# Loading one tile of x ahead of the last chunk of wk, and reordering the first key and query products to match

## The chip, the cores and the metric

The kernel runs on one core of a Trainium2 chip. The metric is the device time of one execution in microseconds (us), less being better. PE is the tensor engine, DVE the vector engine, ACT the scalar engine, and SP the engine that issues most of the DMA loads.

## The reference

A gated mix of two blocks over the same sequence of 2048 rows of width 640. The change touches only the first few microseconds of the attention block: the keys and queries of the first four tiles of 128 rows.

```
qkv = x @ wqkv                       # x 2048x640, wqkv 640x1920, bf16
phi = lambda t: where(t > 0, t + 1, exp(t)) + 1e-6
pq, pk = phi(q), phi(k)              # linear attention with 32 heads of 20
...
return g * a + (1 - g) * b           # g = sigmoid(x . gate_w), b = GeGLU feed-forward
```

The weights wk and wq are 640x640 slices of wqkv. They arrive in five chunks of 128 rows ("chunk 0" to "chunk 4"), because a product over 640 is five accumulated matmuls over 128.

## The kernel before

Loads. `load_xT` is a DMA that transposes a tile of x on its way; `load_wk` and `load_wq` are plain loads of one 160 KB chunk. SP issues in program order, unless `"act"` is given.

```
load_x(0); load_wk(0); load_xT(1); load_wk(3); load_wk(4)
load_wk(1, "act"); load_wk(2, "act")
...                                   # cut: gate weights, by ACT
for i in range(2, NQ):                # NQ = 4: tiles 2 and 3 of x
    load_xT(i)
for k in range(KC):                   # KC = 5
    load_wq(k)
for i in range(NQ, NT):
    load_xT(i)
```

Products. `KM(n, ks)` multiplies tile n by the chunks `ks` of wk, as a 512-wide and a 128-wide matmul per chunk; `QM` does the same with wq (its narrow half is 129 wide, by a gate column that `gate_col()` makes). Products accumulate in PSUM (`ps` in the timelines, where every matmul writes to it). It is used as four slots of two banks; keys of tiles 0 to 3 take slots 0 to 3, and then the queries of tiles 0 to 3 take the same slots again. ACT and DVE turn a finished slot into phi (`phi1`, `phi2`), after which its banks are free.

```
warm(5, 512); warm(1, 128)            # dummy products
...                                   # cut: tile 0 is transposed by PE
warm(2, 128)
for k in range(3): KM(0, [k])
for k in range(3): KM(1, [k])
KM(0, [3]); KM(1, [3])
gate_col()
KM(0, [4]); KM(1, [4])
for n in range(2 * NQ):
    if n in (2, 3):
        KM(n, ALLK)
    if n == NQ:
        for k in ALLK:
            QM(NQ, [k]); QM(NQ + 1, [k])      # two query tiles, chunk by chunk
    if n > NQ + 1:
        QM(n, ALLK)
    phi1(n); phi2(n)
for i in range(NQ, NT):
    KQ(i)                             # the combined key/query stage, tiles 4 to 15
```

One program operation waits for everything it reads at its start: `QM(n, ALLK)` waits for all five chunks of wq, `QM(n, [k])` for chunk k alone.

## Time and profile before

| | before |
|---|---|
| time, median of 6 runs | 274.07 us (273.92 to 274.27) |
| span of the profiled run | 272.6 us |
| first real product | 4.45 us |
| hole before tile 2's keys | 7.55 to 8.12 us |
| queries start | 10.85 us |
| combined stage starts | 16.30 us |

Four lines of the page: the span, PE's busy time, the busy tenths of the DMA engines in 40 slices of 6.8 us, and the chain of work that ended last, by engine.

```profile
span 272.6 us, 3416 instructions
...
PE 267.6 (98%) x1341; PEld 127.9 (47%) x1367; DVE 140.8 (52%) x247; ACT 75.9 (28%) x132; POOL 30.0 (11%) x28
...
DMA  7976999600200011514121221273031110110211
...
PE 96%; DMA 1%; SPq 1%; issue 1%; DVE 0%
```

PE is the bottleneck: 98% busy, and 96% of the chain. The loads of this change fall in the first two slices, where the DMA engines are busy to 70% and over 90%. Summed over shorter stretches, their busy share is 1.09 from 4 to 8 us and 0.91 from 8 to 12 us (a packet is counted where it starts, so a share can exceed 1). A share of about 1 is what "full" means below.

The timeline of PE in the kernel before (start, duration, engine, source line, operation, output from input, count, and in brackets the idle time with what released it). Lines 453 and 454 are the two widths of a key product, 468 and 469 those of a query product, 539 is the combined stage.

```profile
7.00 0.38 PE L453 MATMUL ps<-pool 128*128 128x512 bf16 x1
...
7.27 0.38 PE L453 MATMUL ps<-pool 128*128 128x512 bf16 x1
7.49 0.22 PE L454 MATMUL ps<-pool 128*128 128x128 bf16 x1
8.12 0.39 PE L453 MATMUL ps<-pool 128*128 128x512 bf16 x1 [0.42 <-DMA pool<-in_A_x_dram]
...
10.85 0.38 PE L468 MATMUL ps<-pool 128*128 128x512 bf16 x1
...
16.24 0.22 PE L469 MATMUL ps<-pool 128*128 128x129 bf16 x1
16.30 0.81 PE L539 MATMUL ps<-pool 128*128 128x512 bf16 x3
```

Key products of one chunk start 0.27 us apart. The last one of tile 1 starts its narrow half at 7.49, so tile 2's first would follow at 7.55, but it starts at 8.12: a hole of 0.57 us, ended by a DMA of x. (The bracket says 0.42 because the end that the profile gives a matmul is later than the start of the next: 7.27 + 0.38 = 7.65, against 7.49. I count starts.) From 10.85 the ten chunks of two interleaved query tiles and ten more follow without a hole, 20 x 0.272 = 5.45 us, until 16.30.

SP's queue in the kernel before: the time it takes to issue each load.

```profile
1.71 1.30 SPq L353 DMA_TRANSPOSE pool<-in_A_x_dram  x1
3.06 1.04 SPq L341 DMA_DIRECT2D pool<-in_A_wqkv_dram  x2
4.14 2.53 SPq L353 DMA_TRANSPOSE pool<-in_A_x_dram  x2
6.72 2.48 SPq L341 DMA_DIRECT2D pool<-in_A_wqkv_dram  x5
```

A transposing load takes SP about 1.26 us to issue (two in 2.53), a plain chunk about 0.5 (two in 1.04, five in 2.48).

The landing of a load is the moment at which the last of its 16 semaphore increments is recorded. In the kernel before, in us: wk3 6.37, wk4 6.83, x tile 2 8.07, x tile 3 8.77, wq chunks 0 to 4 at 9.40, 10.13, 10.55, 11.54 and 12.05.

### The profile page before, as it was taken

The page shows a single profiled execution, that of the slowest core. Times are in us where ns is not written, and L with a number is a line of the kernel's source. Part 1 is how long each engine was busy: PE and PEld are TensorE (multiplying, and loading weights), DVE is VectorE, ACT ScalarE, POOL GpSimd, SP SyncE. Part 2 cuts the span into 40 slices and gives each one's busy share as a digit, 9 for nine tenths or more (in the row PEclk, how much of TensorE's full clock was granted, in tenths as well). Part 3 has the DMA queues.
Part 4 walks back from the last instruction along what each step waited for, and adds up shares of the span by engine and source line. Part 5 has one row for each costly group of instructions (what it writes and reads, how often), then busy time and mean ns, then how long its engine had stood idle before and what let it go on. Part 6 is the DMA issues. An engine that isn't in the chain of part 4 may idle for free.

```text
span 272.6 us, 3416 instructions
## 1 busy us (share of the span) xinstructions
PE 267.6 (98%) x1341; PEld 127.9 (47%) x1367; DVE 140.8 (52%) x247; ACT 75.9 (28%) x132; POOL 30.0 (11%) x28
## 2 busy tenths in 40 slices
PE   8999999999999999999999999999999999999997
PEld 3555555544445454444444444444444444444444
DVE  1678989997233335999999999634210000000200
ACT  2455555210422453232222233224011122121021
POOL 5000000003240002242332422000000000000000
DMA  7976999600200011514121221273031110110211
GB/s 192 202 115 127 346 399 388 140 2 19 58 19 2 23 50 51 192 34 49 26 48 25 49 48 27 60 219 105 5 77 38 41 38 19 38 41 19 58 58 41
DMA packets 42864, 23.78 MB, mean 87 GB/s; under 512 B 32223, under 2 KB 41439, under 8 KB 42719
## 3 DMA queue, kind: packets, MB, share of 16 engines
q1 hardware_dynamic: 42517, 23.22, 31.9%
q10 hardware_dynamic: 330, 0.33, 0.3%
q8 instruction: 11, 0.18, 0.3%
q14 instruction: 6, 0.05, 0.1%
HBM read 13.83 MB, written 2.63 MB: 60 GB/s over the span
## 4 chain that ended last, share of the span: by engine, by line
PE 96%; DMA 1%; SPq 1%; issue 1%; DVE 0%
PE ps L700 41%; PE ps L864 23%; PE ps L539 12%; PE ps L596 6%; PE ps L843 4%; PE ps L468 2%; PE ps L811 2%; PE ps L678 2%; PE ps L599 1%; DMA pool<-in_A_x_dram 1%; PE ps L453 1%; PE ps L824 1%; SPq L341 1%; PE ps L721 1%; SPq L353 0%
## 5 line engine op out<-in xcount | busy, mean ns | idle before, releaser
L700 PE MATMUL ps<-pool 128*128 128x512 bf16 x510 | 113.0, 379 | 0.5
L700 PEld LDWEIGHTS ps<-pool 128*128 128x128 bf16 x520 | 50.5, 98 | 60.0
L864 PE MATMUL ps<-pool 128*128 128x512 bf16 (+2 forms) x300 | 62.4, 366 | 0.3
L706 ACT ACTIVATE pool<-ps 128x512 f32<-128x512 f32 x52 | 31.0, 597 | 73.1 <-PE ps L700 73.1
L708 DVE TENSOR_TENSOR pool<-ps,pool 128x512 bf16<-128x512 f32 x52 | 34.7, 689 | 31.7 <-PE ps L700 30.4
L864 PEld LDWEIGHTS ps<-pool 128*128 128x128 bf16 x306 | 29.2, 98 | 33.4 <-issue 0.4
L847 DVE TENSOR_TENSOR pool<-ps,pool 128x512 bf16<-128x512 f32 x4 | 2.8, 690 | 61.5 <-PE ps L843 61.5
L539 PE MATMUL ps<-pool 128*128 128x512 bf16 (+1 forms) x176 | 32.5, 343 | 0.2
L754 POOL TENSOR_TENSOR pool<-pool 128x640 f32<-128x640 bf16 x16 | 22.4, 1404 | 73.0 <-DVE pool L756 65.6
L871 ACT ACTIVATE pool<-ps,pool 128x512 bf16<-128x512 f32 (+1 forms) x16 | 10.9, 680 | 68.6 <-PE ps L864 68.6
L539 PEld LDWEIGHTS ps<-pool 128*128 128x128 bf16 x180 | 17.6, 98 | 15.0
L558 DVE SCALAR_TENSOR_TENSOR pool<-ps,pool 128x128 bf16<-128x128 f32 (+2 forms) x36 | 21.7, 602 | 2.1
L549 ACT ACTIVATE pool<-ps 128x640 bf16<-128x640 f32 x24 | 16.9, 703 | 15.8 <-DVE pool L558 9.3
L596 PE MATMUL ps<-pool 128*128 128x512 bf16 x76 | 19.2, 379 | 0.1
L764 DVE TENSOR_TENSOR pool<-pool 128x640 bf16<-128x640 bf16 x16 | 13.2, 826 | 0.6
L762 DVE TENSOR_SCALAR pool<-pool 128x32 f32<-128x32 f32 x16 | 12.8, 802 | 0.6
L756 DVE TENSOR_REDUCE pool<-pool 128x32 f32<-128x640 f32 x16 | 12.9, 808 | 0.0
L644 DVE TENSOR_TENSOR pool<-pool 128x640 f32<-128x640 f32 x14 | 11.6, 826 | 0.5
L843 PE MATMUL ps<-pool 128*128 128x512 bf16 x51 | 11.5, 379 | 0.1
L646 POOL PARTITION_ALL_REDUCE pool<-pool x1 | 4.0, 3971 | 61.0 <-DVE pool L644 61.0
L596 PEld LDWEIGHTS ps<-pool 128*128 128x128 bf16 x78 | 7.0, 98 | 7.3
L555 DVE TENSOR_SCALAR pool<-pool 128x640 bf16<-128x640 bf16 x24 | 7.9, 327 | 1.7 <-ACT pool L549 0.4
(70 smaller groups left out, 124.1 us busy)
## 6 DMA issues: line engine op xcount, KB each, us to landing
out_dram<-pool SPq DMA_DIRECT2D x19, 128.0 KB, 1.7
pool<-in_B_w_gate_dram SPq DMA_DIRECT2D x1, 2080.0 KB, 14.8
pool<-in_B_w_up_dram SPq DMA_DIRECT2D x1, 2080.0 KB, 18.0
pool<-in_A_wqkv_dram SPq DMA_DIRECT2D x8, 160.0 KB, 3.1
pool<-in_A_x_dram SPq DMA_DIRECT2D x1, 1280.0 KB, 9.2
pool<-in_A_x_dram SPq DMA_DIRECT2D x1, 1120.0 KB, 6.3
pool<-in_B_w_down_dram SPq DMA_DIRECT2D x1, 1120.0 KB, 6.4
pool<-omg_row SPq DMA_DIRECT2D x1, 1024.0 KB, 4.8
```

Source lines behind the costliest of these rows:

```text
L539: last = e.matmul(ps[:, b + p, 0:c1 - c0], xT[:, k, i * 128:(i + 1) * 128], wkq[:, k, c0:c1], start=(k == 0), stop=(k == KC - 1))
L549: P.op("act", lambda e: e.activation(e_buf[m], ps_flat[:, o:o + 640], ACT.Exp), reads=banks, writes=[r_e[m]])
L558: P.op("dve", lambda e, c0=c0, c1=c1: e.scalar_tensor_tensor(dst[:, c0:c1], ps_flat[:, o + c0:o + c1], 1.0 + EPS, e_buf[m][:, c0:c1], ALU. ...
L596: last = e.matmul(ps[:, b, :], pk[i][:, c * 128:(c + 1) * 128], x_aug[:, i, 0:512], start=(i == 0), stop=(i == NT - 1))
L700: last = e.matmul(ps[:, b, :], w[:, k, fc * 128:(fc + 1) * 128], xT[:, k, j * 512:(j + 1) * 512], start=(k == 0), stop=(k == KC - 1))
L706: P.op("act", lambda e: e.activation(ge[n], ps[:, gb, :], ACT.Gelu_apprx_tanh), reads=[bank[gb]], writes=[r_ge[n]])
L708: P.op("dve", lambda e: e.tensor_tensor(hT[fc][:, j * 512:(j + 1) * 512], ps[:, ub, :], ge[n], ALU.mult), reads=[bank[ub], r_ge[n]], write ...
L754: P.op("pool", lambda e: e.tensor_tensor(tmp[n], pq[i], z_b, ALU.mult), reads=[r_pq[i], r_zb], writes=[r_tmp[n]])
L756: P.op("dve", lambda e: e.tensor_reduce(den[n], tmp[n].rearrange("p (h d) -> p h d", h=32), AX.X, ALU.add), reads=[r_tmp[n]], writes=[r_de ...
L764: P.op("dve", lambda e: e.tensor_tensor(pq[i].rearrange("p (h d) -> p h d", h=32), pq[i].rearrange("p (h d) -> p h d", h=32), den[n].unsqu ...
L843: last = e.matmul(ps[:, b, :], wd[:, fc, 512:640], hT[fc][:, j * 512:(j + 1) * 512], start=False, stop=(fc == NFC - 2), skip_group_check=True)
L864: last = e.matmul(ps[:, pb, 0:c1 - c0], lhs, rhs, start=False, stop=(q == len(rows) - 1), skip_group_check=True)
```

## The change

The intent is to have tile 2 of x at hand when PE runs out of work, by loading it ahead of wk's chunk 4, and to do two chunks of tile 2 while chunk 4 is still on its way. The queries of the first two tiles are no longer interleaved.

```diff
             load_wk(3)
+            load_xT(2)
             load_wk(4)
+            load_xT(3)
             load_wk(1, "act")
             load_wk(2, "act")
...
-            for i in range(2, NQ):
-                load_xT(i)
             for k in range(KC):
                 load_wq(k)
...
             gate_col()
+            KM(2, [0, 1])
             KM(0, [4])
             KM(1, [4])
+            KM(2, [2, 3, 4])
             for n in range(2 * NQ):
-                if n in (2, 3):
+                if n == NQ - 1:
                     KM(n, ALLK)
                 if n == NQ:
                     for k in ALLK:
-                        QM(NQ, [k])
-                        QM(NQ + 1, [k])
-                if n > NQ + 1:
+                        QM(n, [k])
+                if n > NQ:
                     QM(n, ALLK)
```

More of the change, by code (lines that the diff above doesn't have):

```diff
@@ L347, in load_x, with load_wk, load_xT @@
                 dma_in(x_aug[:, i, 0:640], A_x[0, i * 128:(i + 1) * 128, :], [r_xn[i]], eng=eng)
-            def load_wk(k, eng="sp", after=()):
-                dma_in(wk[:, k, :], A_wqkv[k * 128:(k + 1) * 128, 640:1280], [r_wk[k]], reads=after, eng=eng)
-            def load_xT(i, after=()):
+            def load_wk(k, eng="sp"):
+                dma_in(wk[:, k, :], A_wqkv[k * 128:(k + 1) * 128, 640:1280], [r_wk[k]], eng=eng)
+            def load_xT(i):
                 P.op("sp", lambda e: e.dma_start_transpose(xT[:, :, i * 128:(i + 1) * 128],
                                                            A_x[0, i * 128:(i + 1) * 128, :]),
-                     reads=list(after), writes=[r_xT[i]], dma=new_dma_key())
+                     writes=[r_xT[i]], dma=new_dma_key())
             def load_wq(k, eng="sp"):
```

## The prediction

> **What bounds the kernel.** TensorE. The page gives PE 98% busy, the chain of waits is 96% PE[...]. From the first real matmul (4.45 us) to the last output PE has one hole worth naming: in the timeline the last key product of tile 1 starts at 7.49 us and should be out in about 0.05, and the first of tile 2 starts at 8.12, released by a DMA of x. That hole is about 0.58 us, 0.2% of the span. After it the key and query matmuls follow at 0.27 us per chunk (a 512-wide and a 128-wide product) until 16.30 us, and nothing later waits for longer than about 0.05. So what moves the start of the combined key/query stage (16.30 us) moves the end by as much.
>
> **What the change does.** No arithmetic is added or removed. SP issues x tile 2's transposing load before wk chunk 4 instead of behind it, tile 3 after chunk 4. SP issue durations in the timeline: a wk chunk 0.43-0.57 us, a transposing load about 1.26. So tile 2 is issued at 3.67 instead of 4.14, chunk 4 at about 4.95 instead of 3.67; tile 3 and wq chunks 0-4 are issued when they were. PE does two chunks of tile 2 (0.54 us) before chunk 4 of tiles 0 and 1 and the other three after; queries of tile 4's slot run alone instead of interleaved with the next one, so wq is consumed at 0.27 us per chunk instead of 0.54.
>
> **Landings now (semaphore landings of the trace), us.** wk3 6.37, wk4 6.83, xT2 8.07, xT3 8.77, wq0-4 9.40, 10.13, 10.55, 11.54, 12.05. DMA engines are near saturated over these microseconds (DMA row 7-9 tenths)[...] (SP's loads land in issue order). So swapping the two should swap about 0.46 us (wk4's step after wk3): estimate xT2 at 7.4-7.7, wk4 at about 8.1 (issue 4.95 plus the 3.16 it took).
>
> **Critical path after.**
> - Gate column ends at 7.0; PE waits for xT2 until about 7.6: a new 0.6 us hole, earlier.
> - Two chunks of tile 2, until 8.15; wk4 is there or nearly.
> - 2 chunks (tiles 0, 1), 3 of tile 2, 5 of tile 3 = 2.7 us: queries start at about 10.8 (10.85 now). Gain 0 to 0.25.
> - Query chunk 4 of the first tile is wanted at about 11.9, before wq4 lands (12.05): a new wait of 0.1-0.3 us. Queries then end at 12.05+0.27+3x1.36 = 16.4 instead of 16.30.
> The hole moves rather than closes. Net about 0, -0.3 to +0.3. ScalarE and VectorE exponentials (0.70 and 1.15 us per tile, against 1.36 of PE) start some 0.9 us later but free banks in time.
>
> **Prediction:** 274.1 us, 80% range 273.7 to 274.5; faster by over 2% 0.01, within 2% 0.98, slower 0.01.
>
> **What would show it.** The hole before tile 2's keys starts near 7.0 and ends at xT2's landing (7.4-7.7); little or no hole before chunk 4 of tile 0; a small wait on a wqkv DMA in the first query tile near 11.8; combined stage starts at 16.2-16.5; unchanged after.
>
> **What would make it wrong.** If xT2 lands by 7.2 and wk4 by 7.8, and wq4 comes earlier than 11.7, up to 0.5 us is gained. If the transposing load delays chunk 4 beyond 8.5, or wq lags more, it loses that much.

The trace of before holds no clock record. The sum came to a net of about 0, -0.3 to +0.3 us, on the 274.07 measured before. That tile 2 and chunk 4 would swap their landings was my estimate, from loads that land in the order of issue in that trace (wk3 6.37, wk4 6.83, x tile 2 8.07).

## The result, and the profile after

| | before | after |
|---|---|---|
| median of 6 runs | 274.07 us | 274.33 us |
| range of fast runs | 273.92 to 274.27 | 274.24 to 274.37 |
| ratio of fast runs, 95% interval | | 1.0008 (0.9995 to 1.0022) |

A ratio is the mean time of one kernel's fast runs over that of the other's fast runs of the same rounds, so it is not quite the ratio of the medians quoted. The change is the same within 2%, and even zero lies inside the interval.

One of the changed kernel's six executions, the profiled one, was slow (284.62 us). Its matmuls of 128x512 in the longest group take 391 ns in place of 379 ns, and the groups of the other stages are slower too. (A clock of 1.0 is given for it, but its trace holds no clock record at all, and time without a record is counted as 1.0.) I explain no time by that run. The profile after is therefore that of the same kernel run again, which is the first experiment, e1_after_again. The two traces agree in the order of the landings and in the places of the waits, but not in their size: in the slow one, queries start at 10.90, wq's chunk 4 lands at 12.15 and PE waits 0.14 us for it, where e1, read below, has 0.70 us of waits for wq. So e1 is one execution, and not the typical one.

The page of the changed kernel: the lines that answer to those of before.

```profile
span 273.2 us, 3416 instructions
...
PE 267.9 (98%) x1341; PEld 127.7 (47%) x1367; DVE 141.0 (52%) x247; ACT 75.9 (28%) x132; POOL 30.0 (11%) x28
...
DMA  7997999500300011523121221263031110110211
...
PE 94%; SPq 3%; DMA 1%; issue 1%; DVE 0%
```

The span is 0.6 us longer in this execution. PE's share of busy time did not move in a visible way, nor did the DMA row; the shares cannot show an effect of this size. The chain gives SP's queue 3% where it was 1%: before, the chain ran back to the load of x tile 2, which SP issued at 4.14 us; now it runs back to the load of wq's chunk 4, issued at 8.83, with more of SP's queue ahead of it.

The timeline of PE in the changed kernel (line 540 is the combined stage now).

```profile
7.03 0.38 PE L453 MATMUL ps<-pool 128*128 128x512 bf16 x1
...
7.30 0.38 PE L453 MATMUL ps<-pool 128*128 128x512 bf16 x1
7.52 0.22 PE L454 MATMUL ps<-pool 128*128 128x128 bf16 x1
8.00 0.39 PE L453 MATMUL ps<-pool 128*128 128x512 bf16 x1 [0.27 <-DMA pool<-in_A_wqkv_dram]
...
10.73 0.38 PE L468 MATMUL ps<-pool 128*128 128x512 bf16 x1
...
11.49 0.22 PE L469 MATMUL ps<-pool 128*128 128x129 bf16 x1
11.74 0.39 PE L468 MATMUL ps<-pool 128*128 128x512 bf16 x1
11.97 0.22 PE L469 MATMUL ps<-pool 128*128 128x129 bf16 x1
12.53 0.39 PE L468 MATMUL ps<-pool 128*128 128x512 bf16 x1 [0.34 <-DMA pool<-in_A_wqkv_dram]
...
16.84 0.22 PE L469 MATMUL ps<-pool 128*128 128x129 bf16 x1
16.90 0.59 PE L540 MATMUL ps<-pool 128*128 128x512 bf16 x2
```

The two chunks of tile 2 start at 7.03 and 7.30, right behind the gate column: tile 2 had landed at 6.87, and there is no wait for it. The hole is now at 7.57 to 8.00 us, before chunk 4 of tile 0, and is ended by a DMA of wqkv. Queries start at 10.73, which is 0.12 us earlier than before. Then they stop twice in the first tile: chunk 3 would follow at 11.55 and starts at 11.74, chunk 4 would follow at 12.02 and starts at 12.53, released by a DMA of wqkv. That is 0.19 + 0.51 = 0.70 us. The combined stage starts at 16.90: 10.73 + 5.45 + 0.70 = 16.88 accounts for it.

SP's queue in the changed kernel.

```profile
1.71 1.31 SPq L353 DMA_TRANSPOSE pool<-in_A_x_dram  x1
3.06 0.57 SPq L341 DMA_DIRECT2D pool<-in_A_wqkv_dram  x1
3.67 1.21 SPq L353 DMA_TRANSPOSE pool<-in_A_x_dram  x1
4.92 0.57 SPq L341 DMA_DIRECT2D pool<-in_A_wqkv_dram  x1
5.54 1.21 SPq L353 DMA_TRANSPOSE pool<-in_A_x_dram  x1
6.79 2.47 SPq L341 DMA_DIRECT2D pool<-in_A_wqkv_dram  x5
```

Tile 2 is issued at 3.67 in place of 4.14, and chunk 4 at 4.92 in place of 3.67. Landings in this trace: wk3 6.20, x tile 2 6.87, wk4 7.96, x tile 3 8.68, wq chunks 0 to 4 at 10.06, 10.54, 10.97, 11.70 and 12.48.

**The end follows the start of the combined stage.** Of every profiled run in the fast state, the device time minus the start of the combined stage is the same: 273.97 - 16.30 = 257.67 before, 274.49 - 16.90 = 257.59 after, and 257.58 to 257.68 in ten of the eleven others (257.82 in e7). So nothing behind the stage reacts to the change, and the start of the stage can be read as the time of the run. That gives a finer measure than the timed rounds, though of one execution each, and the stages below are compared across chips, which the times are not.

### The profile page after: what moved, and what is told of

The parts are those of the page before. It is cut to its first block, busy times and chain, and to the rows that moved or that the text cites. A ratio compares the mean times of both kernels' runs of the same rounds, so it can differ in the third digit from the quotient of the medians.

```text
span 283.4 us, 3416 instructions
## 1 busy us (share of the span) xinstructions
PE 278.7 (98%) x1341; PEld 130.6 (46%) x1367; DVE 142.2 (50%) x247; ACT 76.0 (27%) x132; POOL 30.0 (11%) x28
## 4 chain that ended last, share of the span: by engine, by line
PE 96%; SPq 1%; DMA 1%; issue 1%; DVE 0%
PE ps L701 41%; PE ps L865 23%; PE ps L540 12%; PE ps L597 6%; PE ps L844 4%; PE ps L468 2%; PE ps L812 2%; PE ps L679 2%; PE ps L600 1%; DMA pool<-in_A_wqkv_dram 1%; SPq L353 1%; PE ps L453 1%; PE ps L825 1%; PE ps L722 1%; SPq L341 0%
## 5 line engine op out<-in xcount | busy, mean ns | idle before, releaser
L701 PE MATMUL ps<-pool 128*128 128x512 bf16 x510 | 117.6, 391 | 0.6
L701 PEld LDWEIGHTS ps<-pool 128*128 128x128 bf16 x520 | 51.6, 100 | 63.5
L865 PE MATMUL ps<-pool 128*128 128x512 bf16 (+2 forms) x300 | 64.9, 377 | 0.4
L709 DVE TENSOR_TENSOR pool<-ps,pool 128x512 bf16<-128x512 f32 x52 | 35.8, 689 | 35.3 <-PE ps L701 32.6
L865 PEld LDWEIGHTS ps<-pool 128*128 128x128 bf16 x306 | 29.8, 100 | 35.4 <-issue 0.4
L848 DVE TENSOR_TENSOR pool<-ps,pool 128x512 bf16<-128x512 f32 x4 | 2.8, 692 | 64.2 <-PE ps L844 64.2
L540 PE MATMUL ps<-pool 128*128 128x512 bf16 (+1 forms) x176 | 33.7, 352 | 0.2
L540 PEld LDWEIGHTS ps<-pool 128*128 128x128 bf16 x180 | 17.9, 100 | 15.9
L597 PE MATMUL ps<-pool 128*128 128x512 bf16 x76 | 19.9, 391 | 0.1
L844 PE MATMUL ps<-pool 128*128 128x512 bf16 x51 | 12.0, 391 | 0.1
L597 PEld LDWEIGHTS ps<-pool 128*128 128x128 bf16 x78 | 7.1, 100 | 7.7
```

What stands on the lines that cost most here:

```text
L540: last = e.matmul(ps[:, b + p, 0:c1 - c0], xT[:, k, i * 128:(i + 1) * 128], wkq[:, k, c0:c1], start=(k == 0), stop=(k == KC - 1))
L597: last = e.matmul(ps[:, b, :], pk[i][:, c * 128:(c + 1) * 128], x_aug[:, i, 0:512], start=(i == 0), stop=(i == NT - 1))
L701: last = e.matmul(ps[:, b, :], w[:, k, fc * 128:(fc + 1) * 128], xT[:, k, j * 512:(j + 1) * 512], start=(k == 0), stop=(k == KC - 1))
L709: P.op("dve", lambda e: e.tensor_tensor(hT[fc][:, j * 512:(j + 1) * 512], ps[:, ub, :], ge[n], ALU.mult), reads=[bank[ub], r_ge[n]], write ...
L844: last = e.matmul(ps[:, b, :], wd[:, fc, 512:640], hT[fc][:, j * 512:(j + 1) * 512], start=False, stop=(fc == NFC - 2), skip_group_check=True)
L865: last = e.matmul(ps[:, pb, 0:c1 - c0], lhs, rhs, start=False, stop=(q == len(rows) - 1), skip_group_check=True)
```

## The experiments

Theory: the change moves the hole without shortening the path much, and its small loss comes from wq's chunks 3 and 4, which the tile-by-tile queries want before they land. Rival: the loss is the hole itself, before wk's chunk 4. Second rival: there is no loss, only noise.

All runs in one table. "Stage" is the start of the combined stage in the profiled run, whose time is in the next column. "Half" marks profiled runs in which PE ran at half rate well into the keys, with products of one chunk 0.53 us apart in place of 0.27 (see e3).

| run | median us | before's median, same rounds | ratio, 95% interval | stage us | profiled run us |
|---|---|---|---|---|---|
| e1_after_again | 274.42 | 274.09 | 1.001 (0.9989 to 1.003) | 16.90 | 274.49 |
| e2_queries_paired | 274.67 | 274.09 | 1.0024 (1.0 to 1.0048) | 17.14 | 274.73 |
| e3_queries_alone | 274.55 | 274.09 | 1.0024 (0.9998 to 1.005) | 17.89, half | 275.47 |
| e4_four_ahead | 274.48 | 274.09 | 1.0017 (0.9991 to 1.0042) | 16.59 | 274.18 |
| e5_no_wq_wait | 274.14 | 273.96 | 1.0 (0.9986 to 1.0013) | 17.46, half | 275.14 |
| e6_loads_alone | 274.34 | 273.96 | 1.0011 (0.9998 to 1.0023) | 16.69 | 274.27 |
| e7_wk4_by_act | 274.41 | 273.96 | 1.0011 (0.9998 to 1.0023) | 16.59 | 274.41 |
| e8_queries_alone_2 | 274.31 | 273.88 | 1.0026 (1.0011 to 1.0042) | 16.59 | 274.18 |
| e9_no_wq_wait_2 | 274.38 | 273.88 | 1.0028 (1.0011 to 1.0045) | 16.69 | 274.28 |
| e10_longer_warm | 273.98 | 273.88 | 1.0003 (0.9992 to 1.0015) | 16.64 (its record is missing; from the last query) | 274.22 |
| e11_four_ahead_mixed | 274.32 | 273.88 | 1.0024 (1.0003 to 1.0045) | 16.72 | 274.39 |
| e12_no_wq_wait_two_tiles | 273.99 | 273.65 | 1.0007 (0.9993 to 1.002) | 16.41 | 273.99 |

The experiments ran on three chips, and the median of before moved from 273.65 to 274.09 between sets, so a kernel is compared with the runs of before in its own row. Several of the sets hold one or two executions about 1 us longer than the rest; the ratios contain these.

### e1: the changed kernel again

No edit.

> The changed kernel unaltered, for a trace in the fast state. Theory (pinned by wq): the wait before chunk 4 of wk is gone from the critical path's end because queries are pinned to the landing of wq chunk 4 at about 12.1-12.2 us; the combined stage starts at 12.1+0.27+3x1.36 = about 16.5; time +0.2 to +0.3 us against before. Rival (the moved hole costs): the loss is in the hole before chunk 4 of wk (larger than 0.58 us in the fast state) and the query tile shows no wait. Rival 2 (noise): interval of the ratio contains 1 with five rounds and the combined stage starts at 16.3.

Measured: the six runs lie between 274.27 and 274.50, while eleven runs of before scatter from 273.59 to 275.25. The trace was read above: a wait of 0.70 us in the first query tile, a hole of 0.43 us before wk's chunk 4, and the stage at 16.90, later than the 16.5 that the theory gave, because wq's chunk 4 landed at 12.48. The rival's clause that the query tile shows no wait is refuted by this trace. The timed rounds alone do not exclude noise. The profiled execution, 274.49, is among the slowest of the eleven fast ones of the changed kernel (274.24 to 274.50): less 257.6, the others put the stage at 16.64 to 16.90. The wait of 0.70 us is thus near the upper end, not the usual size.

### e2: the change, but with the two query tiles interleaved as before

```diff
                 if n == NQ:
                     for k in ALLK:
-                        QM(n, [k])
-                if n > NQ:
+                        QM(NQ, [k])
+                        QM(NQ + 1, [k])
+                if n > NQ + 1:
```

> Loads and key order of the change, queries of the first two slots interleaved as before. wq is then consumed at 0.54 us a chunk, so no wait for wq. If the wq wait were all that the change costs, the combined stage starts at about 16.25 and the time is 0.25 us below the changed kernel. My own count says otherwise: the second slot's banks come free only when VectorE finishes tile 1 (11.59 us in the changed trace, against 10.48 before), so PE waits about 0.5 us at 11.1 and the stage starts at about 16.75: +0.45 us against before, 0.2 slower than the changed kernel. So the tile-by-tile queries are what pays for the later exponentials.

The timeline of PE in e2, at the first two query products:

```profile
11.12 0.38 PE L468 MATMUL ps<-pool 128*128 128x512 bf16 x1
11.34 0.22 PE L469 MATMUL ps<-pool 128*128 128x129 bf16 x1
11.95 0.39 PE L468 MATMUL ps<-pool 128*128 128x512 bf16 x1 [0.39 <-DVE pool L492]
```

And that of DVE, the instruction that ends last before 11.95:

```profile
11.07 0.82 DVE L492 SCALAR_TENSOR_TENSOR pool<-ps,pool 128x640 bf16<-128x640 f32 x1
```

PE stands from 11.40 to 11.95 (0.55 us) in front of the second tile's slot, and what releases it is DVE's second instruction for tile 1's keys (11.07 to 11.89). Chunk 4 came late, so the exponentials of tile 1 came late, and the slot with them. The stage starts at 17.14. The wait is what I had counted (0.5 us); the stage is later than my 16.75. It shows what the tile-by-tile queries are for: without them the change trades the wait for wq against a wait for banks. wk's chunk 4 landed 0.39 us later in this execution (8.35) than in e1, so the difference of 0.24 us to e1's stage cannot be put down to the edit; the wait and its releaser can.

### e3 and e8: before, with the queries tile by tile and nothing else

```diff
                 if n == NQ:
                     for k in ALLK:
-                        QM(NQ, [k])
-                        QM(NQ + 1, [k])
-                if n > NQ + 1:
+                        QM(n, [k])
+                if n > NQ:
```

> Before, with only the queries tile by tile. Queries start at 10.85 as before; chunk 4 of wq is wanted at 11.94 and lands at 12.05-12.2: theory pinned by wq expects the combined stage at 16.4-16.55, +0.1 to +0.25 us against before, nearly the whole loss of the change. Rival (the moved hole costs): 0 against before, because nothing of the hole is touched.

The profile of e3 fell on an execution that says nothing of the queries. PE's timeline in it, around the moment at which the rate changes:

```profile
8.55 0.63 PE L453 MATMUL ps<-pool 128*128 128x512 bf16 x1
...
9.15 0.41 PE L453 MATMUL ps<-pool 128*128 128x512 bf16 x1
...
9.46 0.38 PE L453 MATMUL ps<-pool 128*128 128x512 bf16 x1
```

Up to 9.15 us the products of one chunk start 0.53 us apart, and 0.27 after that. wk's chunk 0 had landed at 4.73 us there, against 4.31 in the profile of before, and PE had idled longer ahead of it. The mean clock of the run is given as 1.0 all the same, but only because time without a record counts as full: in e3's trace the records of full clock begin at 9.26 us. In e5 they begin at 8.14, and in the six other traces that have records (e1, e4, e6, e7, e10, e11) at 3.69 to 4.94, each time about where the spacing is 0.27 us from then on. What sets the moment of the change is not shown. That PE's idle time ahead of chunk 0 (0.83 us here, 1.03 in e5) puts it off is a guess: in e11 PE idled 0.77 us there and lost nothing, its products being 0.27 us apart from the first one (4.71) on; its records of full clock begin at 3.69 us, ahead of the idle time.

So the kernel was run again.

> The same kernel as e3_queries_alone, because its profile fell on an execution in which wk chunk 0 landed 0.4 us late and matmuls then ran at half rate until 9.15 us. If the first products run at full rate from about 5.3 us: queries start at 10.85, wait for wq chunk 4 (12.05 to 12.5), stage at 16.4-16.85, with a visible wait on a wqkv DMA in the first query tile; time 0.1 to 0.4 us above before. If there is no wait there: the loss of the change isn't that of the queries.

PE's timeline in e8, at chunk 4 of the first query tile:

```profile
11.99 0.22 PE L469 MATMUL ps<-pool 128*128 128x129 bf16 x1
12.22 0.39 PE L468 MATMUL ps<-pool 128*128 128x512 bf16 x1
```

In e8 wq's chunk 4 landed at 12.17; the query product of chunk 4 started at 12.22 where 12.05 was its turn. That is a wait of 0.17 us at the predicted place, within the range stated. The other 0.11 us of the stage's delay to 16.59 came earlier: tile 2 landed at 8.18 and was taken at 8.23, against 8.12 in before, so queries started at 10.96. (PE ran at half rate until 6.4 us in this execution, 0.53 us a product, and was yet ready for tile 2 at 8.15, just before it landed, so this cost nothing more.) All six runs lie at 274.18 or above, and 274.18 is the highest of before's eleven. Queries alone therefore cost something, on loads that had not been moved. The size isn't settled: the medians differ by 0.43 us, more than the wait in the trace, and two of the six runs (275.25 and 275.51) are of the kind that is 1 us late.

### e4: the change, with four chunks of tile 2 ahead of chunk 4

```diff
-            KM(2, [0, 1])
+            KM(2, [0, 1, 2, 3])
             KM(0, [4])
             KM(1, [4])
-            KM(2, [2, 3, 4])
+            KM(2, [4])
```

> The change, with four chunks of tile 2 ahead of chunk 4 instead of two, which fills the hole before chunk 4 (7.54 to about 8.09 us) with 0.54 us of work. Theory pinned by wq: the hole closes, keys end at about 10.3, and the time is that of the changed kernel within 0.1 us, as the queries wait for wq chunk 4 all the same. Rival (the moved hole costs): 0.5 us faster than the changed kernel, 0.25 faster than before.

PE's timeline in e4, across the place where the hole had been:

```profile
8.16 0.22 PE L454 MATMUL ps<-pool 128*128 128x128 bf16 x1
8.22 0.38 PE L453 MATMUL ps<-pool 128*128 128x512 bf16 x1
```

Measured: the hole before wk's chunk 4 closed; chunk 4 landed at 7.91 and was used at 8.22, without a wait. Yet the queries gained nothing from it. Keys ended at 10.39; the first query waited for its banks until 10.67 (released by DVE), chunk 3 until 11.81 (landed 11.77), chunk 4 until 12.22 (landed 12.18). The median is that of e1 within 0.06 us. The stage, at 16.59, is 0.31 us earlier than in e1, and all of that is explained by wq's chunk 4 landing 0.30 us earlier in this execution. This separates theory and rival: filling the moved hole does not pay, as long as the queries are held back by two things behind it.

### e5, e9 and e12: the change without the wait for wq

These give a wrong result: in the first query tile (e5 and e9, the same kernel) or in the first two (e12), chunks 3 and 4 of wk stand in for those of wq. The matmuls are the same. The comparison with the reference passed all the same; its tolerance does not notice the queries of one or two tiles. (The edit is shown as e12 has it; e5 and e9 do the same for one tile, by a flag.)

```diff
-            def QM(n, ks):
+            def QM(n, ks, true=KC):
...
-                        e.matmul(ps[:, b0, :], lhs, wq[:, k, 0:512], ...)
-                        last = e.matmul(ps[:, b1, 0:129], lhs, wq[:, k, 512:641], ...)
+                        w0 = wq[:, k, 0:512] if k < true else wk[:, k, 0:512]
+                        w1 = wq[:, k, 512:641] if k < true else wk[:, k, 511:640]
+                        ...           # and reads=... names r_wk[k] for r_wq[k] there
-                        QM(n, [k])
+                        QM(n, [k], 3)
-                    QM(n, ALLK)
+                    QM(n, ALLK, 3 if n == NQ + 1 else KC)      # e12 only
```

> Wrong result on purpose: the changed kernel, but chunks 3 and 4 of the first query tile multiply by wk, which is long there, in place of wq. Same matmuls, no wait for wq chunks 3 and 4 in that tile. Theory pinned by wq: the wait there vanishes, the combined stage starts at about 16.25-16.3, and the time falls to that of before, -0.2 to -0.3 us against the changed kernel. Rival (the moved hole costs): unchanged, +0.25 against before.

e5's profile fell on half rate, with products 0.53 us apart until about 8.2 us. Four of its five runs lie between 273.94 and 274.16, and before's nine between 273.75 and 274.72, so the times agree with the expectation; but the trace could not confirm it, and e9, the same kernel, shows below that PE still waits for wq. The agreement is therefore no support for the theory.

> The same kernel as e5_no_wq_wait (wrong arithmetic in one query tile on purpose), for a profile at full rate. Pinned by wq: no wait in the first query tile, the stage starts at 16.3 +- 0.1 us, time equal to that of before within 0.15 us. Moved hole costs: stage at 16.6 or later.

PE's timeline in e9, from the fifth chunk of the first query tile:

```profile
11.92 0.38 PE L470 MATMUL ps<-pool 128*128 128x512 bf16 x1
12.14 0.22 PE L471 MATMUL ps<-pool 128*128 128x129 bf16 x1
12.61 0.38 PE L470 MATMUL ps<-pool 128*128 128x512 bf16 x1 [0.24 <-DMA pool<-in_A_wqkv_dram]
```

The wait left the first tile and came back in front of the second: 12.19 to 12.61, released by a DMA of wqkv (chunk 4 landed at 12.47). I had overlooked that the second tile waits for all five chunks at its start. The experiment did not take the cost away, and its medians (274.38 against 273.88) show none gone. It is a miss in design.

> The changed kernel with chunks 3 and 4 of wk in place of those of wq in the first two query tiles (wrong arithmetic on purpose). e9 took the wait from the first tile alone, and its trace shows it again ahead of the second, at 12.61 us, because that tile waits for all five chunks at once. Here PE needs wq chunks 3 and 4 only at about 13.5 us, after they have landed (12.5 at the latest so far). Pinned by wq: keys of tile 0 and 1 end with chunk 4 of wk at about 8.0+0.54, queries start at about 10.75 and run without a wait; stage at 16.15-16.3, time that of before within 0.15 us and 0.25 to 0.6 us under the changed kernel's. Moved hole costs: a stage still at 16.6 or later.

PE's timeline in e12, across the place where the wait had been:

```profile
11.77 0.38 PE L470 MATMUL ps<-pool 128*128 128x512 bf16 x1
...
12.04 0.38 PE L470 MATMUL ps<-pool 128*128 128x512 bf16 x1
...
12.32 0.38 PE L470 MATMUL ps<-pool 128*128 128x512 bf16 x1
```

With neither tile waiting, queries run from 10.95 at 0.27 us each, and the stage starts at 16.41: 10.95 + 5.45. In e1 it was 16.90. So no wait for wq is left, as the theory expects. The 0.49 us between the two stages isn't the edit alone, however: in e12 wq's chunk 4 landed at 12.27, where PE would have wanted it at about 12.04 (10.95 + 4 x 0.272), so that the wait would have been about 0.3 us in this execution (an estimate from these numbers). The stage is 0.1 us over the range I had given, and for a reason that the trace shows: wk's chunk 4 landed at 8.18 in this execution, and the 10 products between it and the first query take 2.73 us (8.22 to 10.95). The median is 0.34 us above before's, where I had expected 0.15; the ratio of 1.0007 has an interval that contains 1. Against before in the same rounds, that is no better than the changed kernel itself (0.26 and 0.33 us above, ratios 1.0008 and 1.001). So the trace shows the wait for wq removed, but the timed rounds don't show its cost given back, and the cause of the timed loss stays open: chunk 4's late landing can pin the queries at 0.1 us behind before, and more than that I cannot show.

### e6: the loads alone, with PE's order of before

> The loads of the change with PE's order of before. Chunk 4 of wk lands at about 8.1 instead of 6.83, and now all of tile 0 and 1's last products, tile 2 and tile 3 stand behind it: 8.1+0.54+2.72 = 11.36 for the first query, +0.5 us against before (stage at 16.8), with no wait for wq. The wait before tile 2 is gone. If the time is that of before, loads order is not what sets the stage's start and my account is wrong.

The edit is the first two parts of the change's diff alone. PE's timeline in e6, at the gate column and the product after it:

```profile
6.97 0.17 PE L498 MATMUL ps<-pool 128*128 128x5 bf16 x1
7.95 0.39 PE L453 MATMUL ps<-pool 128*128 128x512 bf16 x1 [0.81 <-DMA pool<-in_A_wqkv_dram]
```

PE stands from 7.00 to 7.95 for chunk 4 (landed 7.90), and the stage starts at 16.69, 0.39 us later than before; the median is 0.38 above before's. There is no wait for wq. This is the expected mechanism with the expected size, a little below my 0.5. The order of the loads does set the start of the queries.

### e7: chunk 4 issued by ACT

```diff
-            load_wk(4)
             load_wk(1, "act")
             load_wk(2, "act")
...
             dma_in(gw_sb[0:5, :], ..., [r_gw], eng="act")
+            load_wk(4, "act")
```

> Before, with chunk 4 of wk issued by ScalarE behind the gate weights, so that SP issues tile 2 at 3.67 us and tile 3 and wq some 0.5 us earlier, while chunk 4 is not moved behind tile 2. If issue time on SP is what holds tile 2 back: tile 2 lands at 7.5-7.6, the hole of before (0.58 us) closes, banks are free (tile 1's exponential ends at 10.48), wq lands up to 0.5 us earlier: stage at 15.75-15.85, -0.45 to -0.55 us against before. If the DMA engines are full and bytes are what counts: tile 2 lands at about 8 as before and the time is that of before within 0.1 us.

SP's queue in e7:

```profile
3.06 0.57 SPq L341 DMA_DIRECT2D pool<-in_A_wqkv_dram  x1
3.67 2.52 SPq L353 DMA_TRANSPOSE pool<-in_A_x_dram  x2
6.24 2.48 SPq L341 DMA_DIRECT2D pool<-in_A_wqkv_dram  x5
```

Tiles 2 and 3 and all of wq are issued 0.47 us earlier than before, but tile 2 landed at 8.36 (8.07 before), wq's chunks at 9.54, 9.97, 10.40, 11.53 and 12.01 (9.40 to 12.05 before), and wk3 at 7.16 (6.37 before), which made a new wait of 0.65 us before chunk 3. The stage started at 16.59, 0.29 us later than before, and the median is 0.45 above before's. Neither expectation holds as it stands: nothing was gained, and the time is not that of before within 0.1 us. Nor is it a clean test of issue time on SP: ACT issued chunk 4 at 2.87 us, ahead of wk3 (3.06) and 0.80 us earlier than SP had, and it landed at 6.90 against 6.83 before, while wk3 landed 0.79 later. One load was let past another. What the run shows is that with the DMA engines this full (a share of 1.14 from 4 to 8 us and 1.17 from 8 to 12) earlier issue bought no earlier landing of tile 2 (issued 0.47 us earlier, landed 0.29 later), of wk's chunk 4 (6.90 against 6.83) or of wq's last chunk (12.01 against 12.05).

### e10: before with a longer warm-up

```diff
-            warm(2, 128)
+            warm(8, 128)
```

> Before, with eight dummy 128-wide products instead of two ahead of the first key product, so that PE is not idle while wk chunk 0 is late (0.83 and 1.03 us of idle in the two profiles that ran at half rate until 9.15 and 8.45 us; 0.39 to 0.63 in those that did not). If that idle time is what keeps the rate at half[...]: no execution about 1 us slow any more (before had 275.12 and 275.25 among values of 273.6 to 274.1), a spread under 0.5 us, and a median equal to before's lower values, since up to 0.58 us of delay is absorbed by the wait for tile 2. If the late executions have another cause: the spread of this kernel is that of before.

Five runs between 273.83 and 274.22, none of them slow by 1 us. But the eleven runs of before on the same chip (273.70 to 274.18) had no such execution either, so this says nothing of the half-rate start. Inconclusive.

### e11: four chunks ahead, and queries in a mixed order

On top of e4's edit:

```diff
                 if n == NQ:
-                    for k in ALLK:
-                        QM(n, [k])
-                if n > NQ:
+                    for t, ks in ((0, (0, 1, 2)), (1, (0, 1, 2)), (0, (3, 4)), (1, (3, 4))):
+                        for k in ks:
+                            QM(NQ + t, [k])
+                if n > NQ + 1:
```

> e4_four_ahead, with queries in the order chunks 0-2 of the first slot, 0-2 of the second, 3-4 of the first, 3-4 of the second: wq chunks 3 and 4 are wanted only when they have landed, and the second slot's banks when VectorE has freed them. Counted from e4's trace: first slot from 10.4, second at 11.5, chunk 3 of wq at about 12.3, stage at 16.1-16.25, so 0.3 to 0.4 us below e4 and the changed kernel, and 0.05 to 0.2 below before. If it is no faster than e4, then wq and the banks are not the two things that pin the queries.

Measured: no wait for wq, but queries started at 10.98 where 10.70 was their turn, and once more the second slot stood for DVE until 12.08. wk0 (4.57) and xT1 (6.01) landed late in this execution too. The stage is at 16.72 and five of the six runs lie between 274.07 and 274.41, against a median of 273.88 for before on that chip. No better than before: the exponentials of tiles 0 and 1, which start only when wk's chunk 4 is there, are the third thing that holds the queries.

No version among the twelve beats the kernel before.

## Why the prediction was right, and where it was not

- **The time.** 274.1 us with a range of 273.7 to 274.5 was predicted, and 274.33 measured; the class "within 2%" was given 0.98. Right; but before itself scatters from 273.56 to 275.25 over the sets, so a hit in this range doesn't test the mechanism, and two errors below, a hole put one step too early and a wait put too small, hardly moved it.
- **What bounds the kernel, and how a delay travels.** Right: the stage's start and the time differ by 257.6 us in nearly every profiled run.
- **"PE waits for xT2 until about 7.6: a new 0.6 us hole, earlier."** Wrong. Tile 2 landed at 6.84 to 7.20 in seven of the eight fast traces with the new load order (7.46 in e5), not at 7.4 to 7.7, and PE did not wait for it in e1. I had moved it up by the 0.46 us step of one plain chunk; it came 1.2 us earlier. Its first semaphore increment came 0.67 us earlier (6.69 against 7.36), and the rest is that the other increments followed at once rather than over 0.71 us (see the last section). The hole lies one step later, before chunk 4 (7.57 to 8.00 in e1), which landed at 7.96, near the 8.1 that I gave. As the landing of chunk 4 pins what follows, the start of the queries was still right: 10.73 measured, about 10.8 predicted.
- **"A new wait of 0.1-0.3 us" for wq's chunk 4.** Right in place and kind. It was too small for e1, with 0.51 us for chunk 4 and 0.19 for chunk 3, whose landing I had not seen as late; it fits the slow run (0.14), e8 (0.17) and the estimate for e12 (0.3). The term that was mis-sized is the landing of wq's chunk 4, taken over from before as 12.05. In the eight fast traces with the new loads it was 12.18 to 12.50, mean 12.35; in the four with the old order by SP (before, e3, e8, e10) 12.05 to 12.34, mean 12.16. So the estimate was a little early for the old order too. The 0.2 us between the means is suggested rather than shown: the two ranges overlap, and in the slow run, with the new loads, chunk 4 landed at 12.15.
- **"Combined stage starts at 16.2-16.5."** 16.90 in e1. The changed kernel's fast runs of the first measurement, less 257.6, would put it at 16.64 to 16.77. Late of my range, in e1 by the waits for wq just named.
- **Exponentials keep up.** Right for the change as it is (no wait for banks in e1). e2, e4 and e11 show that the margin is thin: every order of the queries that asked for banks earlier waited for DVE (0.55 us in e2, until 10.67 in e4, until 10.98 in e11).

What came of the change's intent: in e1 the hole of 0.57 us before was replaced by one of 0.43 us, so the queries began 0.12 us earlier, and the tile-by-tile order gave that back, and more, in waits for wq. Even that small gain isn't steady: with the same loads and key order the queries began at 10.73 (e1), 10.83 (e9), 10.90 (the slow run) and 10.95 (e12), against 10.85 before, since they follow the landing of wk's chunk 4. e4 and e12 carry the rest: removing the hole alone does not help, and removing the waits for wq leaves a stage of 16.41 in place of 16.90, part of which is landings. What stays open is the size of the loss in time, and its cause. It is a few tenths of a microsecond, and no interval here separates the changed kernel from the one before.

## What to carry to other kernels

Here, with the DMA engines full (a share of 1.09 from 4 to 8 us in before, 1.01 from 4.4 to 9 in e1), swapping two loads moved a wait from one consumer to the other: 0.57 us before tile 2's keys became 0.43 us before wk's chunk 4 in e1, and 0.95 us in e6. So add up everything that PE needs by then, and look at what the later consumers want next, before counting a gain. The filler that let PE do other work delayed what it overtook, and with it what the overtaken work frees, the exponentials and the PSUM banks of the next products: in e2 DVE finished tile 1 at 11.89 us, and PE stood 0.55 us for its slot. If the time after some point is constant, compare kernels by when they reach that point in their traces, and note how much single landings vary (with one order of loads, 0.3 us for wq's chunk 4 and 0.6 for wk's) before giving a small effect a cause.

## What the traces show and leave unexplained

- The landings follow the order of SP's issue: wk3, x tile 2, wk4, x tile 3 at 6.20, 6.87, 7.96 and 8.68 in e1. What went with the early landing of tile 2: in the thirteen fast traces the 16 increments of x tile 2 came within 0.2 us when a plain load followed it (6.69 to 6.87 in e1, 6.95 to 7.07 in e6) and took 0.4 to 0.8 us when another transposing load did (7.36 to 8.07 in before, 7.46 to 8.18 in e8). What follows is not the whole of it, as the increments of tile 4, which a transposing load always follows, took only 0.20 us in e1 (13.14 to 13.34). Why is not tested.
- In the half-rate start products of one chunk are 0.53 us apart, and 0.27 after it. In e3 a first product delayed by 0.4 us (4.86 against 4.45) went with a change of rate at 9.15 in place of 5.3 us, and with a run of 275.47 us. A mean clock of 1.0 can hide this: e3's records begin only at 9.26 us, and those of before are missing altogether.
